# Raw output weights in the buffers of the segment's inputs, loaded together and split a tile a step

## The chip, the core and the metric

The kernel runs on one core of a Trainium2 chip. A core has a matrix engine (TensorE, "PE" in the profile, with its weight loads as "PEld"), a vector engine (VectorE, "DVE"), a scalar engine (ScalarE, "ACT"), a general engine (GpSimd, "POOL") and a queue engine that here only issues DMAs (SyncE, "SP"). Each runs its own list of instructions in order and waits on semaphores; GpSimd issues some DMAs too. The metric is the device time of one execution in microseconds; the time of a kernel is the median of its runs.

## What is computed

Two attention layers over the same input, mixed by a gate of each row. A has 32 heads with keys and values of their own; B has 32 query heads that share one key and one value head.

```python
x = A_x                                   # 1 x 2048 x 576, 32 heads of 18
g = _sigmoid((x * gate_w).sum(-1, keepdims=True))
a = _A_ref(x, A_wqkv, A_wo)               # softmax(q k^T / sqrt(18)) v, per head, then @ wo
b = _B_ref(x, B_wq, B_wk, B_wv, B_wo)     # the same with one shared k and v, then @ wo
return g * a + (1 - g) * b
```

All arrays are float32. The output projection `@ wo` of both layers is one product here: the 64 heads' outputs, 64 x 18 = 1152 rows, times the two `wo` stacked to 1152 x 576, with the gate already multiplied into the head outputs.

## The kernel before

**Precision.** TensorE works on float32r operands. A float32 value is split into a high part (a cast) and a low part (the value less its high part), and products are sums of high x high, high x low and low x high. `split` (line 236) makes these two parts with one cast and one subtraction on the engines that it is given; in the profile they show as lines 240 and 242. All loads and stores go through `dma` (line 161), by default on SP's queue, and show as line 163.

**The loop.** After a lead-in the program walks 64 heads ("u") with 16 steps of 128 keys each: step T = 16 u + i, from 0 to 1023. In each step `step_scores` (line 736) makes four 128 x 512 blocks of scores and their exponentials on ScalarE, `step_pv` (line 751) multiplies them with the values, and 22 steps ahead (`LEAD`) `step_max` (line 683) takes the row maxima on VectorE for a head to come. `max_rows` (line 706) turns a head's maxima into two rows of its query tile: VectorE reduces and transposes them (`m`, `mt`), GpSimd splits them (`mh`), SP stores them to `m_d` and loads them back into the query tile `qs`. It is called at the start of a block of eight steps, six steps before the head's scores begin: head 46 at step 730 for step 736, head 59 at step 938 for step 944.

**The order of the work** is written out by hand. Strings of letters give the matmuls of eight steps (`PLAIN`, `HALF14`, `TWO12`, `HALF12`, `DENSE`, lines 1153 to 1158); A and B are the halves of "units", projections that run between the score matmuls on the two halves of the array. A model of the clock (`Clock`, line 48) picks the PSUM bank of each. At every second step `begin` (line 1162) starts what `when` (line 1037) has put down for that step and then takes one piece of the first generator in the list `slow`, or two pieces in some stretches of steps; at steps with T % 16 = 10 it takes none. The pieces are GpSimd's and SP's work that runs along: `normalise` (line 803) divides a tile of 128 rows of head outputs by the sums, four column blocks of 512, and stores it in high and low parts (`on_d`); `prep_wo` (line 864) loads the rows of the output weights and splits them.

**Steps that matter here.** Row units, which project the rest of the queries and keys, run from step 226 (`RB`) to 730 (`RE`), one in eight steps; their raw inputs (`xst`) stand in two buffers each of the tags `oih` and `oil`, and `cut_x` (line 553) splits them on GpSimd a unit ahead. The output projection (`out_proj`, line 878) runs in three segments: tiles 0 to 3 from step 730 (units from 738 on, the last one just ahead of 930), tiles 4 to 7 from step 942 (units from 946), and tile 8 at the end. Its inputs, 256 columns of four tiles in high and low parts, are loaded into the same tags `oih` and `oil` (line 889). The split weights of both first segments share the tiles `woh` and `wol`. `SEG` (line 1064) says for each of the two when `prep_wo` and when `out_proj` is begun; `prep_wo` is put in front of what is in `slow`.

In the kernel before `prep_wo` has one raw buffer of 128 x 576, `wost`, and goes tile by tile: load, next piece, split, next piece. The tag `wost` also serves `half_step` (line 942) as `tmp`, the buffer between ScalarE's copy of a unit's first half and GpSimd's add (lines 968 to 976) in the second segment. `normalise` of tile 5 is put into `slow` at step 693 and that of tile 7 at 917.

Of the kernel before, what the change touches and what calls it, by code (L numbers as in the profile page):

```python
# [8 lines left out]
F32 = mybir.dt.float32  # L9
# [9 lines left out]
D = 576  # L19
# [137 lines left out]
def gated_mix_kernel(ctx: ExitStack, tc: tile.TileContext, xT, wall, wv, wo, out):  # L157
    nc = tc.nc
    P = 128

    def dma(o, i, eng=None):
        o, i = (x.bitcast(F32) if x.dtype == F32R else x for x in (o, i))
        return (eng or nc.sync).dma_start(o, i)  # L163
# [72 lines left out]
    def split(src, h, l, eng_h, eng_l):  # L236
        if eng_h is nc.scalar:
            nc.scalar.activation(h, src, AF.Copy)
        else:
            eng_h.tensor_copy(h, src)  # L240
        if l is not None:
            eng_l.tensor_tensor(l, src, h.bitcast(F32), op=OP.subtract)  # L242
# [253 lines left out]
    L = {("kd", 0): kdb}  # L496
# [209 lines left out]
    def max_rows(u, eng=nc.gpsimd):  # L706


        m = ms[u % 2]
        clk.other(MAXED)  # L710
        nc.vector.tensor_reduce(m[:, 0:16], MX.pop(u), axis=AX.X, op=OP.max, negate=True)
        mt = lead.tile([P, 32], F32, name="mt")
        nc.vector.transpose(mt, m)  # L713
        mh = lead.tile([P, 2, 32], F32R, name="mh")
        split(mt, mh[:, 0, :], mh[:, 1, :], eng, eng)
        md = m_d[u % 4]
        dma(md, mh.rearrange("p a f -> p (a f)"))
        for b in (SB, MB) if u > NU - 3 else (SB,):
            for a in range(2):
                dma(qs[u % 3][b + 54 + a:b + 55 + a, :].rearrange("o (i b f) -> o i b f", b=4, f=32),  # L720
                    md.rearrange("(b i) (o a f) -> o a i b f", i=32, o=1, a=2)[:, a, 0:16])
# [142 lines left out]
    def prep_wo(t0, rows):  # L864
        nt = len(rows)
        w = {y: L["pool"].tile([P, nt, D], F32R, name=f"wo{y}", tag=f"wo{y}{nt}") for y in "hl"}
        for i, r in enumerate(rows):
            t = t0 + i
            st = L["pool"].tile([P, D], F32, name="wost")
            if FIRST_ROW[t]:  # L870
                dma(st[:DH], wo[DH * (NU - 1):DH * NU, :])
            dma(st[FIRST_ROW[t]:r], wo[P * t:P * t + r - FIRST_ROW[t], :])
            yield
            split(st[:r], w["h"][:r, i, :], w["l"][:r, i, :], nc.gpsimd, nc.gpsimd)
            yield
        WO[t0] = w

# [159 lines left out]
    def when(T, f):  # L1037
        at.setdefault(T, []).append(f)
# [22 lines left out]
    when(RB - 8, lambda: (early("px"), begin_units(row_units())))  # L1061
    RE = RB + 8 * 7 * (MT - NT)
    when(RE, open_oacc)
    SEG = ((0, [P] * 4, 450, RE), (4, [P] * 4, 930, 942))
    for t0, rows, Ta, Tb in SEG:
        when(Ta, lambda t0=t0, rows=rows: slow.insert(0, prep_wo(t0, rows)))
        when(Tb, lambda t0=t0, rows=rows: begin_units(out_proj(t0, rows, first=t0 == 0)))
    when(908, lambda: slow.append(prep_wo(8, [P])))
    when(980, load_gates)

# [91 lines left out]
    def begin(T):  # L1162

        for f in at.get(T, []) + at.get(T + 1, []):
            f()
        if slow and T % 16 != 10:
            for _ in range(2 if T > 1000 or 914 < T < 946 else 1):
                if slow:
                    try:
                        next(slow[0])  # L1170
                    except StopIteration:
                        slow.pop(0)
# [3 lines left out]
    def emit(ops, units=0):  # L1176
        for op in ops.replace(" ", ""):
            if op == "s":
                if pos["s"] % 8 == 0:
                    begin(pos["s"] // 4)  # L1180
# [48 lines left out]

    open_ph2()  # L1230
    begin(0)
    emit("x")
    while pos["s"] < 4 * (NSTEP - LEAD):
        T = pos["s"] // 4
        if (T + LEAD) % 16 == 0 and (T + LEAD) // 16 - 1 < NU:
            max_rows((T + LEAD) // 16 - 1, nc.gpsimd if T > 16 else nc.vector)
        if T >= SEG[1][3] + 4:
            emit(DENSE, 4)
# [52 lines left out]
```

## Time and profile before

| | us |
|---|---|
| median of 3 runs | 2639.51 |
| lowest, highest run | 2637.39, 2640.74 |
| the profiled execution | 2640.37 |
| its span, first to last instruction | 2638.6 |

A row of the profile's lists reads: line of the program, engine, operation, tile written <- tile read, shapes, count, then busy time, mean in ns of one, and the engine's idle time in front of it with what ended it ("<-"). In a timeline the start and the length come first and the idle time stands in brackets. A queue is marked by a q (SPq). The granted clock is TensorE's, 1.00 at full speed; busy times of TensorE are modelled ends of pipelined matmuls, and two matmuls on the halves of the array overlap.

### The profile page before, as it was taken

How to read it: one execution, taken by the hardware profiler on the slowest of the kernel's cores; microseconds unless marked ns; L12 is line 12 of the kernel's file. 1: busy time of each engine (PE TensorE's matmuls, PEld its weight loads, DVE VectorE, ACT ScalarE, POOL GpSimd, SP SyncE). 2: the span in 40 equal slices, each digit the busy share in tenths (PEclk: the TensorE clock that was granted, in tenths of full speed). 3: DMA queues.
4: the chain of work that ended last, by engine and by line, in shares of the span. 5: the costliest groups of instructions: out<-in, count | busy, mean ns of one | idle time of the engine just before them, and what ended most of it. 6: DMA issues, size and time to landing. Idle time of an engine off the chain costs nothing.

```text
span 2638.6 us, 66897 instructions
## 1 busy us (share of the span) xinstructions
PE 2624.3 (99%) x25213; PEld 1405.2 (53%) x25213; DVE 2397.0 (91%) x4575; ACT 2447.3 (93%) x4862; POOL 850.5 (32%) x1087
## 2 busy tenths in 40 slices
PE   9999999999999999999999999999999999999999
PEld 7655545545455455554554545545555545445665
DVE  6899999999999999999999999999989999998883
ACT  5999999999999999999999999999999999998887
POOL 3611000211365535645555356444200020013113
PEclk9999999999999999999999999999999999999999
DMA  8412111212343234323534444444422332134312
GB/s 249 143 56 63 37 48 56 76 51 71 98 119 108 90 98 119 114 87 111 160 124 134 124 132 148 135 123 116 138 85 73 102 100 83 55 95 123 103 57 92
DMA packets 176328, 270.28 MB, mean 102 GB/s; under 512 B 58905, under 2 KB 137193, under 8 KB 164625
## 3 DMA queue, kind: packets, MB, share of 16 engines
q1 hardware_dynamic: 159813, 212.70, 28.1%
q0 software_dynamic: 15152, 51.79, 5.3%
q8 instruction: 198, 3.24, 0.5%
q10 hardware_dynamic: 1040, 1.52, 0.2%
q14 instruction: 125, 1.02, 0.1%
HBM read 190.26 MB, written 66.90 MB: 97 GB/s over the span
## 4 chain that ended last, share of the span: by engine, by line
PE 97%; DMA 2%; POOL 0%; DVE 0%; ACT 0%; issue 0%; ACTq 0%; SPq 0%; DVEq 0%
PE acc L755 38%; PE bank L695 29%; PE bank L740 17%; PE bank L956 11%; DMA xs<-xT 1%; PE bank L278 1%; PE acc L767 1%; PE bank L936 1%; PE bank L1108 0%; DMA wost<-wo 0%; DMA xsh<-xT 0%; POOL wol L242 0%; POOL oacc L929 0%; DVE mx L704 0%; ACTq L163 0%
## 5 line engine op out<-in xcount | busy, mean ns | idle before, releaser
L748 ACT ACTIVATE pt<-bank 128x512 f32<-128x512 f32 x4096 | 2146.2, 616 | 125.8 <-PE bank L740 72.9
L704 DVE TENSOR_REDUCE mx<-bank 128x1 f32<-128x512 f32 x3002 | 1886.6, 683 | 122.2 <-PE bank L740 63.6
L740 PE MATMUL bank<-qs,ksb 56*128 56x512 f32 x2688 | 907.3, 424 | 0.4 <-DVE mx L704 0.4
L695 PE MATMUL bank<-ksb,qs 54*128 54x512 f32 x2270 | 806.8, 426 | 0.0
L755 PE MATMUL acc<-pt,vb 128*19 128x256 f32 (+3 forms) x6144 | 553.1, 455 | 0.0
L695 PEld LDWEIGHTS bank<-ksb,qs 54*128 54x128 f32 x2270 | 383.1, 184 | 319.2 <-ACT pt L748 190.5
L755 PE MATMUL acc<-pt,vg 128*19 128x512 f32 (+3 forms) x5952 | 535.9, 456 | 0.0
L740 PEld LDWEIGHTS bank<-qs,ksb 56*128 56x128 f32 x2688 | 441.6, 184 | 154.2 <-DVE mx L704 64.4
L740 PE MATMUL bank<-qs,ksa 56*128 56x512 f32 x1408 | 467.7, 426 | 2.1 <-DMA qs<-m_d 2.1
L695 PE MATMUL bank<-ksa,qs 54*128 54x512 f32 x1232 | 440.2, 427 | 0.0
L701 DVE CUSTOM_DVE_ANT_0 junk<-bank,xb 128x512 bf16<-128x512 f32 x500 | 342.7, 685 | 29.7 <-PE bank L740 24.5
L698 ACT ACTIVATE xb<-bank 128x512 f32<-128x512 f32 x500 | 292.4, 606 | 13.8 <-PE bank L740 4.9
L695 PEld LDWEIGHTS bank<-ksa,qs 54*128 54x128 f32 x1232 | 208.3, 185 | 151.3 <-ACT pt L748 87.5
L240 POOL CAST mh<-mt 128x32 fp32r<-128x32 f32 x62 | 13.0, 210 | 839.1 <-DVE mt L713 616.9
L740 PEld LDWEIGHTS bank<-qs,ksa 56*128 56x128 f32 x1408 | 226.1, 185 | 86.7 <-DVE mx L704 30.6
L755 PEld LDWEIGHTS acc<-pt,vb 128*19 128x19 f32 x6144 | 123.4, 97 | 203.1 <-issue 169.6
L755 PEld LDWEIGHTS acc<-pt,vg 128*19 128x19 f32 x5952 | 120.1, 98 | 207.4 <-issue 181.5
L240 POOL CAST rhl<-rst 128x292 fp32r<-128x292 f32 (+2 forms) x81 | 34.0, 420 | 478.5 <-issue 283.8
L956 PE MATMUL bank<-xr,wrh 64*128 64x292 f32 (+1 forms) x1134 | 168.0, 300 | 0.0
L695 PE MATMUL bank<-kdb,qs 54*128 54x512 f32 x372 | 159.8, 430 | 0.0
L956 PEld LDWEIGHTS bank<-xr,wrh 64*128 64x128 f32 x1134 | 139.5, 186 | 2.8
L558 POOL TENSOR_TENSOR xr<-xst,xr 128x876 fp32r<-128x876 f32 (+1 forms) x63 | 130.4, 2070 | 0.0
(171 smaller groups left out, 2398.9 us busy)
## 6 DMA issues: line engine op xcount, KB each, us to landing
qs<-qk SPq DMA_DIRECT2D x366, 144.0 KB
xst<-xT SPq DMA_DIRECT2D x54, 438.0 KB
ksa<-qk SPq DMA_DIRECT2D x132, 144.0 KB
qk<-rhl POOLq DMA_DIRECT2D x54, 292.0 KB, 4.4
ksb<-qk SPq DMA_DIRECT2D x60, 144.0 KB
qk<-phl POOLq DMA_DIRECT2D x16, 512.0 KB, 5.3
onh<-oh POOLq DMA_DIRECT2D x32, 256.0 KB, 3.9
onl<-ol POOLq DMA_DIRECT2D x32, 256.0 KB, 4.5
```

What stands on the lines that cost most here:

```text
L240: eng_h.tensor_copy(h, src)
L278: nc.tensor.matmul(fp[:, p0:p0 + g], w[a][:kr, k, :], X[b][:kr, k, x0 + p0:x0 + p0 + g], start=(n == 0), stop=(n == len(PROJ) - 1))
L558: nc.gpsimd.tensor_tensor(x[:, 5:8, 0:n], t0, x[:, 0:3, 0:n].bitcast(F32), op=OP.subtract)
L695: nc.tensor.matmul(pm, qs[u % 3][b:b + 54, i * P:(i + 1) * P], k, start=True, stop=True)
L698: nc.scalar.activation(MX["x", u, i], pm, AF.Relu)
L701: nc.vector.tensor_tensor_reduce(junk, pm, MX.pop(("x", u, i)), 1.0, -3e38, op0=OP.add, op1=OP.max, accum_out=MX[u][:, i, c:c + 1])
L704: nc.vector.tensor_reduce(MX[u][:, i, c:c + 1], pm, axis=AX.X, op=OP.max)
L740: nc.tensor.matmul(ps, kst(u)[b:b + 56, i * P:(i + 1) * P], qs[u % 3][b:b + 56, c * 512:(c + 1) * 512], start=True, stop=True)
L748: nc.scalar.activation(pt, ps, AF.Exp, scale=SCALE)
L755: nc.tensor.matmul(acc[32 * j:32 * j + 19, a:b], v_of(u, i), PT[u, i, j][:, a:b], start=(i == 0), stop=(i == 15), skip_group_check=True)
L767: nc.tensor.matmul(acc[32 * j:32 * j + 19, 256 * half + a:256 * half + b], v_of(NU - 1, i), pt[:, x + a:x + b], start=(i == 0), stop=(i == ...
L956: nc.tensor.matmul(u.fp[op][:, 0:u.n], x[b:b + 64], y[b:b + 64], start=(n == 0), stop=(n == last))
```

## The change

`prep_wo` is split into a loading piece and one splitting piece a tile. For the segments of four tiles the raw rows go into the four buffers of the inputs (tags `oih`, `oil`, two each) in place of the one buffer `wost`, and all four loads are issued in the first piece. The segment of one tile keeps `wost`. The first segment's `prep_wo` moves from step 450 to step 722 (`RE - 8`), in front of the pieces of tile 5's normalisation; the second one's stays at 930. The stretch in which `begin` takes two pieces ends at step 930 in place of 946. With that the second segment's pieces fall on the steps 930 (loads), 932, 934, 936 and 940 (splits), the first segment's on 722, 724, 726, 728 and 732.

```diff
     def prep_wo(t0, rows):
         nt = len(rows)
         w = {y: L["pool"].tile([P, nt, D], F32R, name=f"wo{y}", tag=f"wo{y}{nt}") for y in "hl"}
+        ST_ = []
         for i, r in enumerate(rows):
             t = t0 + i
-            st = L["pool"].tile([P, D], F32, name="wost")
+            if nt == 1:
+                st = L["pool"].tile([P, D], F32, name="wost")
+            else:
+                st = L["pool"].tile([P, 4, 256], F32, name="wost4", tag=f"oi{'hl'[i % 2]}", bufs=2) \
+                    .rearrange("p k f -> p (k f)")[:, 0:D]
             if FIRST_ROW[t]:
                 dma(st[:DH], wo[DH * (NU - 1):DH * NU, :])
             dma(st[FIRST_ROW[t]:r], wo[P * t:P * t + r - FIRST_ROW[t], :])
-            yield
-            split(st[:r], w["h"][:r, i, :], w["l"][:r, i, :], nc.gpsimd, nc.gpsimd)
+            ST_.append(st)
+        yield
+        for i, r in enumerate(rows):
+            split(ST_[i][:r], w["h"][:r, i, :], w["l"][:r, i, :], nc.gpsimd, nc.gpsimd)
             yield
         WO[t0] = w
...
-    SEG = ((0, [P] * 4, 450, RE), (4, [P] * 4, 930, 942))
+    SEG = ((0, [P] * 4, RE - 8, RE), (4, [P] * 4, 930, 942))
...
-            for _ in range(2 if T > 1000 or 914 < T < 946 else 1):
+            for _ in range(2 if T > 1000 or 914 < T < 930 else 1):
```

## The prediction

> **What bounds the kernel now.** I read the page first, then the waits of the matmul engine, the chain of waits around the one that is left, and the windows over the same place.
>
> ```profile
> span 2638.6 us, 66897 instructions
> PE 2624.3 (99%) x25213; PEld 1405.2 (53%) x25213; DVE 2397.0 (91%) x4575; ACT 2447.3 (93%) x4862; POOL 850.5 (32%) x1087
> ```
>
> TensorE is busy for all but 14 us, GpSimd for a third. So moving work on GpSimd or in the DMA queue is worth something only where TensorE stands still for it. The list of its waits has one such entry of over 2 us:
>
> ```profile
> PE bank L740 <- DMA qs<-m_d: 2.1, 1, 2.1
> ```
>
> The chain of waits (start, length, what; us) says where that wait comes from:
>
> ```profile
> 2382.03 1.43 POOL wol L242
> 2383.48 2.85 DMA wost<-wo
> ...
> 2388.58 3.35 DMA wost<-wo
> ...
> 2394.18 2.73 DMA wost<-wo
> 2396.95 0.68 POOL woh L240
> 2397.70 1.43 POOL wol L242
> 2399.36 0.26 POOL mh L242
> 2399.64 1.45 DMA m_d<-mh
> 2401.10 0.59 SPq L163
> 2401.75 2.18 DMA qs<-m_d
> 2404.07 0.47 PE bank L740
> ```
>
> This is the second segment's weights, at steps 930 to 936. They share one raw buffer, so a load waits for the split before it, and GpSimd waits for the load. Behind the fourth split stands, on the same engine, the split of head 59's negated row maxima (mh), which goes through DRAM into the last rows of that head's queries; its first score matmul (step 944) starts at 2404.07, after 2.08 us of waiting.
>
> The clock shows a second loss. The windows' columns: length, then busy PE, PEld, DVE, ACT, POOL, then granted clock, DMA share, GB/s.
>
> ```profile
> 2402.00:2404.00 2.00, 0.00 (x0) 0.00 (x0) 0.47 (x1) 0.93 (x2) 1.42 (x2) 1.00 0.35 81
> 2404.00:2406.00 2.00, 1.94 (x20) 0.84 (x20) 1.30 (x3) 1.09 (x2) 1.98 (x4) 0.74 0.99 342
> 2406.00:2408.00 2.00, 2.00 (x17) 0.86 (x13) 0.78 (x2) 0.68 (x2) 0.82 (x1) 0.50 1.09 313
> 2408.00:2410.00 2.00, 2.00 (x28) 0.98 (x30) 1.62 (x3) 1.44 (x4) 0.00 (x0) 0.91 0.62 245
> ```
>
> After the idle stretch the clock falls to 0.74, 0.50 and 0.91 of full for 2 us each: 2 x (0.26 + 0.50 + 0.09) = 1.70 us of work not done. Together 2.08 + 1.70 = 3.78 us.
>
> A check without the clock column: two plain blocks of eight steps follow each other here, and the same matmuls can be found in both.
>
> ```profile
> 2381.92 0.85 PE L755 MATMUL acc<-pt,vg 128*19 128x128 f32 x16
> 2388.32 0.49 PE L695 MATMUL bank<-ksa,qs 54*128 54x512 f32 x1
> 2400.47 0.84 PE L755 MATMUL acc<-pt,vg 128*19 128x128 f32 x16
> 2410.60 0.50 PE L695 MATMUL bank<-ksa,qs 54*128 54x512 f32 x1
> ```
>
> In the undisturbed block the second lies 6.40 us behind the first, in the disturbed one 10.13 us: 3.73 us lost. It isn't regained: the first block with projection units takes 23.26 us (2410.60 to 2433.86), a later one 23.11.
>
> ```profile
> 2433.86 0.49 PE L695 MATMUL bank<-ksb,qs 54*128 54x512 f32 x1
> 2445.33 1.63 PE acc L755 x24
> 2468.44 1.64 PE acc L755 x24
> ```
>
> **The change part by part.** *Second segment, four loads at once (step 930).* No instruction is added: four loads and eight split instructions as before. What goes is three waits for a load between splits. The rows for the new order:
>
> ```profile
> 2360.60 0.29 PE L956 MATMUL bank<-wol,oih 64*128 64x288 f32 x1
> 2375.14 19.36 SPq L163 DMA_DIRECT2D wost<-wo  x4
> 2381.29 0.66 POOL L240 CAST woh<-wost 128x576 fp32r<-128x576 f32 x1 [17.96 <-PE bank L740]
> 2388.85 0.21 DVE L713 STREAM_TRANSPOSE mt<-m 128x32 f32<-128x32 f32 x1
> ```
>
> The four buffers of the inputs are last read by the first segment's last unit, whose last matmul starts at 2360.60; SP comes to the loads at 2375.14, so none of them has to wait for a buffer. The first split starts 6.15 us after the issue (2381.29) and stays there. A split takes 0.74 us from cast to subtract and 1.43 us for the subtract, 2.17 in all. In the new order mh comes before the fourth split (it belongs to step 938, that split to 940, since no weight step runs at 938). For the landing of the loads in flight together there is no row, so bounds: if all land with the first, the third split ends at 2381.29 + 3 x 2.17 = 2387.8, before DVE has delivered mt at 2388.85 + 0.21 = 2389.06, and mh starts at once; if they come one after another at the longest 3.35 us of the chain, the third lands at 2387.99 and its split ends at 2390.16. From the end of the last split to the matmul the chain takes 2404.07 - 2399.13 = 4.94 us. So the row is there at 2394.0 or 2395.1, and TensorE, which went idle at 2404.07 - 2.08 = 2401.99, has 6.9 us to spare at the worse end. I take all of the 3.73 us as gained. What is late next on SP's queue, the segment's first input load, stands behind the same row and moves up with it; the fourth split ends by about 2394.5 and the first unit runs after 2410 - 3.73.
>
> [...]
>
> *One split a step instead of two (steps 930 to 944).* The rest of tile 7's normalisation, which had double steps up to 944, comes later and singly, 20 us or so; of it, inputs of the segment are made that are read from step 955 on. That order stays right: the block of columns read then is written at step 944, the next at 952 for step 971.
>
> *First segment, moved from step 450 to 722.* At 450 TensorE lost nothing by it, so leaving gains nothing:
>
> ```profile
> 1193.00:1237.00 44.00, 44.00 (x426) 22.07 (x424) 41.69 (x79) 42.02 (x85) 22.83 (x27) 1.00 0.44 130
> ```
>
> At the new place the rows of SP and POOL, and of head 46's first score:
>
> ```profile
> 1859.86 0.54 SPq L163 DMA_DIRECT2D sum_d<-oe  x1
> 1869.28 0.43 POOL L240 CAST rhl<-rst 128x296 fp32r<-128x296 f32 x1 [12.70 <-DVE rst L931]
> 1875.29 0.21 POOL L240 CAST mh<-mt 128x32 fp32r<-128x32 f32 x1 [2.33 <-DVE mt L713]
> 1875.86 0.35 SPq L163 DMA_DIRECT2D m_d<-mh  x1
> 1888.26 0.40 PE L740 MATMUL bank<-qs,ksb 56*128 56x512 f32 x1
> ```
>
> SP issues the loads after 1860.4 and is then free until 1875.86. With the 6.15 us of above the first lands at 1866.6; two splits end at 1870.9, 1.6 us later than the last row unit's split starts now; that unit's rows are wanted only near the end. The third split (2.17) comes behind it and ends near 1875, where mh waits for DVE anyway. If it were late: 1875.29 to the landing of the row is about 5 us as above, so 1888.26 leaves 8 us. The fourth comes behind mh. Cost 0; without this cover, each microsecond beyond 8 would be one of TensorE and then the clock's 1.70. Tile 5's normalisation, pushed back by six steps, feeds the second segment, far later.
>
> **The sum.** 0 (step 450) + 0 (step 722) - 3.73 (step 930) + 0. The profiled execution took 2640.37 us around its 2638.6, so 2636.6 for one like it; against the median 2639.51, **2635.8 us**.
>
> **The rivals.**
>
> *The clock's share stays* (gain 2.08, time 2637.4). [...] Against it: no other 20 us window before the last one shows a clock under 1.00.
>
> *The change doesn't do what it says* (2639.5): the loads crowd each other so that the third split still ends near 2397 and the wait stays. For it: the first load already needs 6.15 us. Against it: it would need 7 us more than the worse bound.
>
> *Slower: the adds of the second segment wait for the rest of tile 7's normalisation.* A unit's first half is copied by ScalarE to one buffer (tmp), freed by GpSimd's add; what the change puts off now runs between these adds.
>
> ```profile
> L976 POOL TENSOR_TENSOR oacc<-tmp,oacc x28: 797/806/816, 2415.1 to 2572.7; 128x288 f32<-128x288 f32 x28
> 2400.69 1.30 POOL L850 TENSOR_TENSOR ot<-ot,R 128x512 f32<-128x512 f32 x1
> 2402.35 0.61 POOL L240 CAST oh<-ot 128x512 fp32r<-128x512 f32 x1 [0.36 <-DMA onh<-oh]
> 2403.19 1.26 POOL L242 TENSOR_TENSOR ol<-ot,oh 128x512 fp32r<-128x512 f32 x1 [0.24 <-DMA onl<-ol]
> 2404.40 0.58 POOL L163 DMA_DIRECT2D onh<-oh  x1
> ```
>
> Two column blocks at 1.30 + 0.61 + 1.26 + 2 x 0.58 = 4.33 and the two issues of a third, 1.16: 9.82 us. If all of it reached TensorE: 2639.51 - 3.73 + 9.82 = 2645.6. Against it: adds come every (2572.7 - 2415.1) / 27 = 5.84 us and take 0.81; a piece of normalisation is at most 1.87 and its waits 0.60. It decides only where a piece holds an add up by more than 5.84 - 0.81 = 5.0 us, twice what these rows give.
>
> **How the numbers follow.** About 0.2% (5.3 us: below 2634.2, above 2644.8) is what a measurement of this kernel can tell from no change. Forecast 0.70, the clock's share 0.14, no effect 0.09, slower 0.07. The forecast lies 1.6 us above the bound for faster, and one of the three runs lay 2.1 us under its median: I give 0.20 of the 0.70 to faster, the rest to within. The slower case lies just over its bound; 0.05 of its 0.07 goes there, 0.02 to within. So faster 0.20, within 0.75, slower 0.05. The range: from the forecast less a bit more than that run's 2.1, 2633.3, to no effect plus the 1.23 of the highest run, 2640.7.
>
> **What would show it.** Right: TensorE's list has no wait for qs from m_d; the clock is 1.00 from 2400 to 2410; one group of four weight loads on SP within some 3 us at each segment; the splits follow each other at 2.17 us; the pair of matmuls above is 6.4 us apart in both plain blocks; nothing new at 1860 to 1890. Wrong: a wait of the score matmul near 1888 or 2402, ScalarE's tmp copy waiting for the adds, or the clock falling without an idle stretch.

## The result

| | before | after |
|---|---|---|
| median of 20 runs, us | 2639.18 | 2635.52 |
| lowest, highest, us | 2636.17, 2642.00 | 2633.67, 2637.93 |
| span of the profiled execution, us | 2638.6 | 2632.0 |

The kernel is 3.66 us faster: ratio 0.9986, 95% interval 0.998 to 0.9992. That is a gain by its interval (2.1 to 5.3 us), though within the 0.2% that the prediction called no change. The forecast was 2635.8.

The page of the kernel after:

```profile
span 2632.0 us, 66889 instructions
PE 2621.7 (100%) x25213; PEld 1404.5 (53%) x25213; DVE 2395.4 (91%) x4575; ACT 2447.6 (93%) x4862; POOL 850.5 (32%) x1087
```

TensorE has the same 25213 matmuls, GpSimd the same busy time. The two spans differ by 6.6 us, more than the medians, and that has to be taken apart before anything is read from it. A good landmark is VectorE's copy of a finished head's sums (line 779, `head_out`), once for each head. The timeline of VectorE for heads 0, 57 and 58, first before, then after (start, length):

```profile
136.81 0.69 DVE L779 COPY oe<-acc 128x512 f32<-128x512 f32 x1 [0.15 <-PE acc L755]
...
2369.92 0.69 DVE L779 COPY oe<-acc 128x512 f32<-128x512 f32 x1 [0.18 <-PE acc L755]
...
2410.73 0.69 DVE L779 COPY oe<-acc 128x512 f32<-128x512 f32 x1
```

```profile
134.25 0.69 DVE L779 COPY oe<-acc 128x512 f32<-128x512 f32 x1 [0.15 <-PE acc L755]
...
2367.09 0.69 DVE L779 COPY oe<-acc 128x512 f32<-128x512 f32 x1 [0.32 <-PE acc L755]
...
2404.28 0.69 DVE L779 COPY oe<-acc 128x512 f32<-128x512 f32 x1
```

Before is behind by 2.56 us at head 0, by 2.83 at head 57, and by 6.45 at head 58. The 2.56 arise in the lead-in, which the change doesn't touch. Over the next 57 heads, the first segment's old and new place among them, 0.27 us are added. Then one head's stretch, from 57 to 58, is 40.81 us before and 37.19 after: 3.62 us, in the one place that the prediction named. This stretch serves as the measure in all that follows. The prediction's own pair of matmuls says the same: 10.13 us apart before, 6.39 after (2397.75 to 2404.14).

There GpSimd and SP run so after (timelines):

```profile
2378.48 0.66 POOL L240 CAST woh<-wost 128x576 fp32r<-128x576 f32 x1 [17.86 <-DMA wost<-wo]
2379.22 1.42 POOL L242 TENSOR_TENSOR wol<-wost,woh 128x576 fp32r<-128x576 f32 x1
2380.58 0.67 POOL L240 CAST woh<-wost 128x576 fp32r<-128x576 f32 x1
2381.33 1.42 POOL L242 TENSOR_TENSOR wol<-wost,woh 128x576 fp32r<-128x576 f32 x1
2382.69 0.67 POOL L240 CAST woh<-wost 128x576 fp32r<-128x576 f32 x1
2383.44 1.42 POOL L242 TENSOR_TENSOR wol<-wost,woh 128x576 fp32r<-128x576 f32 x1
2386.41 0.21 POOL L240 CAST mh<-mt 128x32 fp32r<-128x32 f32 x1 [1.55 <-DVE mt L713]
```

```profile
2372.11 3.03 SPq L163 DMA_DIRECT2D wost<-wo  x4
2386.98 0.33 SPq L163 DMA_DIRECT2D m_d<-mh  x1
2388.58 1.24 SPq L163 DMA_DIRECT2D qs<-m_d  x2
```

Four loads are issued within 3.03 us in place of 19.36; the splits follow each other at 2.1 us with no wait between them, and now it is GpSimd that waits 1.55 us for VectorE's mt. TensorE's list of waits has no entry for qs; this is its head:

```profile
PE bank L409 <- DVE ones L200: 1.9, 1, 1.9
PE bank L1115 <- DVE mx L1125: 1.5, 2, 1.0
PE acc L767 <- DVE oe L999: 0.5, 1, 0.5
```

The first two are of the `warm` matmuls and the lead-in, the third of the end. The clock stays at 1.00 where it fell before (windows, after):

```profile
2402.00:2404.00 2.00, 2.00 (x29) 0.92 (x18) 2.00 (x4) 1.98 (x5) 0.00 (x0) 1.00 0.47 147
2404.00:2406.00 2.00, 2.00 (x25) 1.80 (x22) 2.00 (x4) 2.00 (x5) 0.00 (x0) 1.00 0.52 164
```

At the first segment's new place two splits lie before the last row unit's split (`rhl`) and the third behind it, the order that was worked out. They come sooner than worked out: the first starts 3.14 us after the issue at 1858.10 and not 6.15, so the row unit's split isn't held up but waits 1.03 us for VectorE. Head 46's mh still waits for VectorE and not the other way round (GpSimd's timeline, after):

```profile
1861.24 0.66 POOL L240 CAST woh<-wost 128x576 fp32r<-128x576 f32 x1 [10.42 <-DMA wost<-wo]
...
1863.37 0.66 POOL L240 CAST woh<-wost 128x576 fp32r<-128x576 f32 x1
...
1866.56 0.43 POOL L240 CAST rhl<-rst 128x296 fp32r<-128x296 f32 x1 [1.03 <-DVE rst L938]
...
1868.94 0.68 POOL L240 CAST woh<-wost 128x576 fp32r<-128x576 f32 x1
...
1872.57 0.21 POOL L240 CAST mh<-mt 128x32 fp32r<-128x32 f32 x1 [1.45 <-DVE mt L713]
```

### The profile page after: what moved, and what is told of

It is laid out like the page before. It is cut to its first block, busy times and chain, and to the rows that moved or that the text cites. A ratio compares the mean times of both kernels' runs of the same rounds, so it can differ in the third digit from the quotient of the medians.

```text
span 2632.0 us, 66889 instructions
## 1 busy us (share of the span) xinstructions
PE 2621.7 (100%) x25213; PEld 1404.5 (53%) x25213; DVE 2395.4 (91%) x4575; ACT 2447.6 (93%) x4862; POOL 850.5 (32%) x1087
## 4 chain that ended last, share of the span: by engine, by line
PE 98%; DMA 1%; DVE 0%; ACT 0%; SPq 0%; POOL 0%; issue 0%; ACTq 0%; DVEq 0%
PE acc L755 39%; PE bank L695 29%; PE bank L740 17%; PE bank L963 11%; PE bank L278 1%; PE bank L1115 0%; PE bank L943 0%; DMA xsh<-xT 0%; PE acc L767 0%; DMA R<-r_d 0%; SPq L163 0%; POOL oacc L936 0%; DMA wst<-wall 0%; PE bank L1017 0%; DMA sm<-sum_d 0%
## 5 line engine op out<-in xcount | busy, mean ns | idle before, releaser
(171 smaller groups left out, 2397.0 us busy)
```

## The experiments

### One part at a time

The first, second and fourth edit are shown against the kernel after, the third against the kernel before; "..." stands for lines left out.

**The second segment alone.** `prep_wo` takes the four buffers and the single steps for tiles 4 to 7 only; tiles 0 to 3 keep one buffer, at step 450.

```diff
-            if nt == 1:
+            if t0 != 4:
                 st = L["pool"].tile([P, D], F32, name="wost")
...
+            if t0 != 4:
+                yield
+                split(st[:r], w["h"][:r, i, :], w["l"][:r, i, :], nc.gpsimd, nc.gpsimd)
+                yield
...
-    SEG = ((0, [P] * 4, RE - 8, RE), (4, [P] * 4, 930, 942))
+    SEG = ((0, [P] * 4, 450, RE), (4, [P] * 4, 930, 942))
```

> The second segment alone is changed: its four loads go at once into the four input buffers at step 930, one split a step; the first segment stays at step 450 with its one raw buffer. Theory (all of the gain is head 59's row of maxima, which stood behind the second segment's splits on GpSimd): the whole gain, 3.7 us under before, 2635.5; no wait of TensorE for qs from m_d, clock 1.00 from 2400 to 2410. Rival (the first segment's move gives part of it, by taking GpSimd's waits out of the row units): clearly less than 3.7, down to 0.

Measured: 2635.52 us against 2639.16 before in the same set, ratio 0.9989 (0.998 to 0.9997); no wait for qs, and 37.06 us from head 57 to head 58. All of the gain that can be told from the scatter is here.

**The first segment alone**, moved to step 722 with four buffers, the second as before with its double steps.

```diff
-            if nt == 1:
+            if t0 != 0:
                 st = L["pool"].tile([P, D], F32, name="wost")
...
-            for _ in range(2 if T > 1000 or 914 < T < 930 else 1):
+            for _ in range(2 if T > 1000 or 914 < T < 946 else 1):
```

> The first segment alone is changed: its four loads go at once at step 722, one split a step; the second segment keeps its one raw buffer and its double steps at 930 to 944. Theory: nothing, 2639.2, with the 2.1 us wait near 2404 and the clock's dip after it as before. Rival (the move gives part): 1 to 3.7 us under before.

Measured: 2639.27 us against 2639.16, ratio 0.9998 (0.9989 to 1.0007): nothing, as expected. But the profile held a surprise. The wait is there, the fall of the clock behind it (from here on, the dip) is not (waits, then windows of this kernel; columns as in the prediction):

```profile
PE bank L740 <- DMA qs<-m_d: 2.0, 1, 2.0
```

```profile
2402.00:2404.00 2.00, 1.06 (x12) 0.58 (x16) 0.52 (x1) 0.50 (x2) 1.93 (x3) 1.00 0.69 207
2404.00:2406.00 2.00, 2.00 (x34) 0.93 (x26) 1.65 (x5) 1.36 (x4) 1.70 (x2) 1.00 1.00 327
2406.00:2408.00 2.00, 2.00 (x26) 0.86 (x18) 2.00 (x4) 2.00 (x5) 0.00 (x0) 1.00 0.82 256
```

The stretch from head 57 to 58 is 39.37 us here, 2.18 over the kernel after where the kernel before lost 3.62. So either the dip is not in every execution, or the move does away with it; the profiles at the end of this section settle that.

**One buffer, four steps earlier.** The kernel before with one number changed.

```diff
-    SEG = ((0, [P] * 4, 450, RE), (4, [P] * 4, 930, 942))
+    SEG = ((0, [P] * 4, 450, RE), (4, [P] * 4, 926, 942))
```

> The kernel before with one number changed: the second segment's weights begin at step 926 in place of 930. One raw buffer, loads and splits in turn and the double steps stay. Theory (what counts is where head 59's split stands in GpSimd's queue, not how many loads are in flight): the first split waits on GpSimd for the first segment's last matmul near 2361 and the chain of three more ends near 2390, about when mt comes (2389); head 59's row is there near 2395, before 2402, so the whole gain, 2635.5. Rival (it takes the loads in flight together): the wait of TensorE stays, 2637.4 to 2639.2.

Measured: 2634.98 us, ratio 0.9987 (0.9978 to 0.9996), no wait for qs from m_d, 37.07 us from head 57 to 58. GpSimd's timeline:

```profile
2360.71 0.66 POOL L240 CAST woh<-wost 128x576 fp32r<-128x576 f32 x1 [4.25 <-PE bank L740]
...
2375.88 0.67 POOL L240 CAST woh<-wost 128x576 fp32r<-128x576 f32 x1 [13.00 <-DMA wost<-wo]
...
2380.95 0.66 POOL L240 CAST woh<-wost 128x576 fp32r<-128x576 f32 x1 [2.90 <-DMA wost<-wo]
...
2385.93 0.66 POOL L240 CAST woh<-wost 128x576 fp32r<-128x576 f32 x1 [2.81 <-DMA wost<-wo]
...
2392.91 0.21 POOL L240 CAST mh<-mt 128x32 fp32r<-128x32 f32 x1
```

GpSimd still waits 23 us in front of these four splits, and it costs nothing: the fourth split begins 11 us earlier than before (about 10 when the two executions are lined up at head 57), and mh runs at 2392.91 in place of 2399.06. It came 3 us later than expected, behind two pieces of normalisation, and that too was free. So the gain needs neither four buffers nor loads in flight together; it needs head 59's split to come in time.

**Double steps back.** The kernel after with `914 < T < 946`.

> The kernel after, with the stretch of double steps back at 946: splits two a step, and the rest of tile 7's normalisation earlier and faster. Theory: no difference to the kernel after, 2635.5; mh comes some 3 us later than there, behind the fourth split and a piece of normalisation, with 4 us still to spare. Rival (putting the normalisation off costs something in the second segment): 1 us or more below the kernel after.

Measured: 2635.95 us, ratio 0.9988 (0.9979 to 0.9997); stretch 37.22 against 37.19. mh starts at 2389.55, 3.1 us later than after. Neither putting the normalisation off nor pulling it forward makes a difference that these runs can tell.

### How much room there is, and what a wait costs

In the kernel after, head 59's split on GpSimd is repeated; each repeat writes the same values and makes the row later.

```diff
-        split(mt, mh[:, 0, :], mh[:, 1, :], eng, eng)
+        for _ in range(13 if u == 59 else 1):
+            split(mt, mh[:, 0, :], mh[:, 1, :], eng, eng)
```

> The kernel after; head 59's split on GpSimd (mh from mt) is made 13 times in a row in place of once, which makes its row later by 12 x 0.49 = 5.9 us. Theory: in the kernel after the row is ready near 2391.4 and TensorE wants it near 2399.2 (its step 944), 7.8 us later, so 5.9 us cost nothing: 2635.5, no wait, clock 1.00. Rival (the margin is smaller than worked out, the change only just got rid of the wait): a wait for qs from m_d again and 1 us or more lost.

> The same 18 times: 17 x 0.49 = 8.3 us later, 0.6 us beyond the margin. Theory of the wait: TensorE waits 0.6 us. For the clock: if it falls after any idle stretch, 0.6 + 1.7 us lost, 2637.8; if only after a long one, 0.6 us lost, 2636.1, clock 1.00 throughout.

> The same 21 times: 20 x 0.49 = 9.8 us later, 2.0 us beyond the margin, the wait of the kernel before made again by another cause. Theory: a wait of about 2.1 us and the clock's dip of 1.7 us behind it: 3.7 us lost, 2639.2, as before. Rival (the dip isn't tied to the idle stretch, or the kernel before lost by something else too): 2 us lost, 2637.5, clock 1.00 after the wait.

> The same 27 times: 26 x 0.49 = 12.7 us later, 5.0 us beyond the margin. Theory: a wait of 5.0 us and a dip of the clock that is not longer than after 2.1 us (1.7 us): 6.7 us lost, 2642.2. Rival (the dip grows with the idle stretch): 2 x 1.7 us or more on top of the wait, 2644 and over.

A repeat takes 0.61 us and not 0.49 (13 of them start between 2389.7 and 2397.0), so the doses were larger than meant. Measured, in us, with the delay taken from the trace (first to last start of the repeated cast); the before of this set stands at 2639.83:

| splits | delay | wait of TensorE | clock at half around the wait | stretch 57 to 58 over after's 37.19 | median |
|---|---|---|---|---|---|
| 13 | 7.3 | 0.26 | none | 0.47 | 2636.41 |
| 18 | 10.3 | 3.21 | 6.84 | 5.48 | 2640.85 |
| 21 | 12.1 | 5.08 | 10.24 | 9.21 | 2642.90 |
| 27 | 15.8 | 8.69 | 10.24 | 11.48 | 2647.38 |

The first row sets the room: 7.3 - 0.26 = 7.0 us. With that the other waits follow: 10.3 - 7.0 = 3.3, 12.1 - 7.0 = 5.1, 15.8 - 7.0 = 8.8. What was expected of the first dose holds nearly (the room was 7.0, not 7.8). The cost of a wait doesn't hold: the dip is not a fixed 1.7 us. After the longest wait it is the rival set down there that holds, a dip that grows with the wait (10.24 us at half after 8.69 of waiting, 3.40 after the 2.08 of before; 2644 and over expected, 2647.38 measured). The windows with 18 splits:

```profile
2400.00:2402.00 2.00, 0.61 (x3) 0.17 (x3) 0.99 (x2) 1.55 (x4) 1.98 (x4) 0.96 0.14 49
2402.00:2404.00 2.00, 0.18 (x2) 0.21 (x4) 0.00 (x0) 0.00 (x0) 1.06 (x1) 0.50 0.76 202
2404.00:2406.00 2.00, 2.00 (x16) 0.83 (x20) 1.30 (x3) 1.08 (x2) 0.00 (x0) 0.50 1.04 345
2406.00:2408.00 2.00, 2.00 (x18) 0.83 (x6) 0.36 (x1) 0.26 (x1) 0.00 (x0) 0.50 0.83 243
2408.00:2410.00 2.00, 2.00 (x26) 0.86 (x22) 1.68 (x4) 1.50 (x4) 0.00 (x0) 0.83 0.58 196
```

In windows of 0.5 us the clock of these traces is 1.00 or 0.50 in all but those in which it changes (before: 0.96 from 2404.5, 0.50 from 2405.0 to 2408.0, 0.62 from 2408.0, then 1.00). So a window of 2 us at mean c holds 2 x 2 x (1 - c) us of half: 0.16 + 2 + 2 + 2 + 0.68 = 6.84 us. The same sum in the prediction's windows of before gives 3.40, and 10.24 in the two longest waits. What falls into the wait itself is left out of the price: with 18 splits TensorE resumes at 2403.82, and the half speed up to 2408.68 costs 2.4 us; with the 3.21 of waiting that is 5.6, against 5.48 measured.

The row of 21 splits must be read with care, for each stretch is of one execution. Its ten runs fall into two groups, seven from 2642.40 to 2643.20 us and three from 2644.67 to 2644.86, and the profiled one (2644.67) is of the three. The 9.21 us are its price; by the medians, 2642.90 against 2635.52 of the kernel after in another set, the usual price is about 7 us.

### Is the dip the kernel's or the execution's?

The kernel before was profiled three times more, the first-segment-only kernel once.

> The kernel before, unchanged, profiled once more, since the first-segment-only kernel showed the same wait (1.95 us) with no dip of the clock after it. [...] Rival (the dip belongs to the kernel before, and the first segment's move took it away): the dip in each of the three profiles.

> [...]

> [...]

> The kernel with the first segment alone changed, profiled once more: four of four profiles of the kernel before show the dip of the clock behind the wait, the one of this kernel none. [...] Rival (the first segment's move takes the dip away): a wait of about 2 us, clock 1.00 behind it and 2.2 us between those heads, once more. No dip would leave it open, a dip refutes the rival.

| kernel | wait | clock at half | stretch 57 to 58 over after |
|---|---|---|---|
| before (of the prediction) | 2.1 | 3.40 | 3.62 |
| before, again | 2.4 | 3.40 | 3.95 |
| before, again | 2.5 | 3.40 | 4.06 |
| before, again | 1.9 | 3.44 | 3.47 |
| first segment alone | 2.0 | none | 2.18 |
| first segment alone, again | 2.3 | 3.44 | 3.99 |

Waits and windows of the last:

```profile
PE bank L740 <- DMA qs<-m_d: 2.3, 1, 2.3
```

```profile
2404.00:2406.00 2.00, 0.47 (x4) 0.33 (x4) 0.00 (x0) 0.17 (x1) 1.75 (x3) 1.00 0.38 102
2406.00:2408.00 2.00, 2.00 (x20) 0.53 (x17) 1.30 (x3) 1.09 (x2) 1.98 (x3) 0.57 1.03 346
2408.00:2410.00 2.00, 2.00 (x18) 1.09 (x18) 1.17 (x2) 1.08 (x3) 0.29 (x1) 0.57 1.01 298
```

The three of before alone would have spoken for the rival, which expected the dip in each of them. The last profile refutes it: the first-segment-only kernel shows the dip too, 4 x (0.43 + 0.43) = 3.44 us. So the dip belongs to the execution. Length alone doesn't decide it either: a wait of 1.92 us had it, one of 1.95 had not.

What does decide was not shown. The runs show only where the clock fell. Before, it fell at 2404.96, 0.89 us after TensorE had resumed at 2404.07. With 18 splits it fell at 2401.84 (2408.68 - 6.84), within the wait, 1.2 us after its start at 2400.61 (2403.82 - 3.21); these times are estimates from the windows above, since the ends of matmuls are modelled. In the execution without a dip the wait lies from 2400.99 to 2402.94, and the clock is 1.00 in every window of 2 us from 2398 to 2412.

## Why the prediction was right

*What bounds and what is gained.* The 3.73 us were measured from one execution of before, by the distance of two matmuls; the stretch between heads gives 3.62 in the same execution, the medians 3.66. That the medians come within 0.1 us is partly luck: their interval allows a gain of 2.1 to 5.3. Undoing each part showed that the second segment has all of it.

*Where it comes from.* That mh is what has to come in time, and not the loads themselves, was argued from the order on GpSimd; the one-buffer kernel at step 926 shows it, by the same gain with 23 us of waiting left on GpSimd.

*The new order's times.* First split after the issue: 6.15 us taken, 6.37 measured (2378.48 - 2372.11). A split 2.17, measured 2.1. mh at once after mt: so it was, the better of the two bounds. Room at TensorE: 6.9 to 8 us by the two bounds, 7.0 by the repeated splits. With mh at the better bound it should have been 8; the way from mh's last start to the matmul took 5.8 us with 13 splits (2397.02 to 2402.83), not the 4.94 taken, and what made it longer stays open.

*What was costed at nothing.* Leaving step 450, coming to 722, the single steps: the first-segment-only and the double-steps kernels show no difference that their intervals can tell.

*The clock's share.* The prediction had it as a rival, with 0.14, that it would not be bought back. A single execution can do without the dip, as the first profile of the first-segment-only kernel did (1.95 us of waiting, no half speed behind it), but five of six profiles had it, behind waits of 1.9 to 2.5 us. The unprofiled runs fit: of the 60 runs of before in the two sets of experiments eight show a mean clock of 1.000, and these are the five and the three shortest of their sets (2636.39 to 2637.33 us, medians 2639.16 and 2639.83). So at least some runs go without the dip, most don't, and the median carries nearly the whole. A gain of 2.2 us would have been the answer for the sixth profile.

*The slower rival.* The adds of the second segment do run between the pieces put off, and the room worked out for them (5.0 us against pieces of 2.5) was enough: the whole stretch of 58 to 62 keeps its distance to before, 6.45 us at head 58 and 6.78 at head 62. ScalarE's copy to tmp in that segment has no wait for GpSimd in the list of waits, only 1.6 us in all for TensorE, as before.

## What to carry to other kernels

On an engine that is idle two thirds of the time (GpSimd here, 32% busy, which waited 23 us at no cost in the one-buffer kernel at step 926) a wait is free until something with a due time stands behind it in the same queue: look for that instruction, work out its room, and moving the waiting work a few steps may do as much as new buffers. Price a stall of TensorE by the distance of two landmarks across it and not by the idle time alone, for the clock can add to it: here 1.5 us to a wait of 2.1 (before) and 4.1 to one of 5.1 (21 splits, profiled execution). And before spans of two profiles are compared, line them up by a landmark that repeats; here 2.6 of 6.6 us had nothing to do with the change.

## What the runs showed of the hardware

The half-speed stretches around the waits lasted 3.40 or 3.44 us (five profiles with waits of 1.9 to 2.5 us), 6.84 (18 splits, 3.21 of waiting) and 10.24 (21 and 27 splits, 5.08 and 8.69). Two waits of nearly equal length ended differently: one of 1.92 us had a dip behind it, one of 1.95 had none.

Not expected was the price of a longer wait. In the profiled executions one of 3.2 us cost 5.5 us, one of 5.1 cost 9.2 (about 7 in most runs), one of 8.7 cost 11.5: for each microsecond of waiting TensorE lost 1.7, 1.8 and 1.3.

The scatter between runs of one kernel (some 4 to 6 us) arises in part before head 0. In the four profiles of before the first landmark lies between 135.22 and 136.81 us and keeps its distance to head 57 within 0.7. The code is the same up to there in all kernels of this study, yet the profiled execution with 13 splits has its first landmark 3.40 us later than that of the kernel after, and is still 3.32 us later at head 57. In it the clock stood at half from 118.26 to 121.67, in the lead-in; by half of that length, an estimate, that is up to 1.7 of the 3.40 us.
